# A state-space layer with a shift-mixing MLP on one core: the second mixing product from float16 halves, and a new order of the work

## The chip, the core and the metric

The kernel runs on one NeuronCore of one Trainium2 chip. The metric is device microseconds of one execution, lower is better. The kernel before takes 673.48 us (median of 3 runs, 673.35 to 673.55).

TensorE (PE) multiplies matrices, VectorE (DVE) and ScalarE (ACT) do the elementwise work, SyncE (SP) issues the transfers. Each engine works off its own instructions in order and waits on semaphores for the others.

## The reference, cut to what matters

The input is 2048 positions of 512 channels. It is normed, goes through two branches, and their product is added to it:

```
xn = layernorm(u)
# branch A: a long convolution (2048 taps for each channel)
K[d, l] = Re sum_n C[d,n] * dt[d]*B[d,n] * exp(dt[d]*A[d,n]*l)     # n = 0..127
s = irfft(rfft(pad(xn)) * rfft(pad(K))) + xn * Dskip
# branch B: shift mixing, then an MLP
h  = gelu(layernorm(xn) @ w1)          # 512 x 512
hs = concat(h quarter 0 shifted +1, 1 by -1, 2 by +2, 3 by -2) @ w2
x1 = xn + hs
h2 = gelu(layernorm(x1) @ w3) @ w4     # 512 x 1376, 1376 x 512
out = u + s * silu(x1 + h2)
```

## The kernel before

The 2048 positions stand as 16 slots of 128 in X, [128, 16, 512] float32 in SBUF.

**Branch A.** `tables(hf)` makes the powers that K is summed from. For each of 8 blocks a half (`block`, `waves`, `factors`), ACT computes exponentials (`mag`) and sines, and DVE turns them into products: `kt` and `pt` name the tables, first angles (TENSOR_SCALAR kt<-pt rounds to whole turns, pt<-kt,pt subtracts them), then sines, then sines times magnitudes. The last step are two multiplications by `mag` of each of `kt` and `pt`. Each pair of tables feeds PE: 256 small matmuls into bank pc (pc<-kt and pc<-pt, 32 weight columns, 64 wide; `sums`). What the tables of a half give is copied out (`kev`), goes through `kstage1` (k1e, to a scratch in HBM) and `products`, which reads the two spectra back (`kin`, `uin`), transforms them, multiplies them on DVE (`kh`, `pr`) and transforms back (`z1e`); the transform of u is `u_stage1` (`ue`). The last stages (`inverse`, `finish`) read a scratch as `zin`.

**Branch B.** `token_mixing` has 8 pairs of slots. `x_pair` norms and transposes two slots into xT; `h_pair` multiplies by w1 in float32 (16 matmuls of 256 columns a pair, into pb, with one gelu for each half) into hT. `hs_pair` multiplies the shifted h by w2, float32, 4 matmuls of 512 columns a slot (64 in all), into bank pa, and DVE adds that to X. The quarters of slots that wrap around are copied into `hw` by `wrapped`.

**MLP.** `mlp(g)` works on the two slots of group g, for g = 0 to 7. w3 and w4 are scaled by a power of two (found from sums of squares, `weight_squares`, `pow2_scale`) and split by `prep` into two float16 halves; the activations are split too, and each product is three float16 matmuls (high by high, and the two crossed). `mlp_input` norms two slots (x1n), transposes and splits them (x1T); then come six steps of w3 (pb<-x1T,w3h, 24 matmuls of 256 columns), gelu into g32, the split into ghl (ACT or DVE the high half, DVE the low half) and w4 (pa<-w4h,ghl, 12 matmuls of 512 columns).

**What sets the order.** No line of the program stands where it runs. All instructions are recorded into a `Plan` with what they read and write, and a due number (`due`: a stage's number, from the constants M0, H0, Q0, KA and so on, plus that stage's entry of the table SHIFT). `Plan.order` then walks a clock with modelled costs and takes for each engine, among what is ready in that model, the lowest due number. `E.affine` and `E.copy` may go to ACT or to DVE, by PREFER, AVOID and that clock. The order is fixed when the program is built; each engine's queue is what it gives, and all instructions carry the line of `issue`, L310.

**Places.** The weights' staging buffer `wst` is one buffer of 4 KB a partition: each of the 12 blocks of w3 and w4 is loaded into it once for its sum of squares and once more for `prep`. `stile` hands out the blocks that hold w1 and the eight pairs of h, `wtile` the four buffers that x2, x1n and g32 share, `vtile` two for xT and x1T.

Of the kernel before, what the change touches and what calls it, by code (L numbers as in the profile page):

```python
# [125 lines left out]
)  # L126
Q0, QC = -778.0, 0.05
SWITCH = 2279.26
PREFERP, AVOIDP = 2674.41, 272.51
PREFER, AVOID = 3332.92, 790.65  # L130
PV, T0, TC = 257.0, 396.7, 309.52
LX, LC, LP, LW, LV = -4000.0, 0.11, -3964.6, -2693.7, -3696.7
# [1117 lines left out]
```

## Time and profile before

| | before |
|---|---|
| median of 3 runs | 673.48 us |
| the profiled execution | 674.49 us |
| its span | 672.7 us |
| PE, DVE, ACT busy in it | 93%, 80%, 71% |
| granted clock of TensorE, mean | 0.97 |

The span is what the trace's instructions take from the first to the last; 1.8 us of the profiled execution lie around it, and it is 1.0 us above the median. Busy time is the share in which an engine has an instruction under way. Durations on DVE are recorded from an instruction's begin to its end, and the next one can begin before that end. A float32 matmul has two records in the trace, a float16 one or a transpose one, so the counts of records are not those of instructions.

### The profile page before, as it was taken

The page shows a single profiled execution, that of the slowest core. Times are in us where ns is not written, and L with a number is a line of the kernel's source. Part 1 is how long each engine was busy: PE and PEld are TensorE (multiplying, and loading weights), DVE is VectorE, ACT ScalarE, POOL GpSimd, SP SyncE. Part 2 cuts the span into 40 slices and gives each one's busy share as a digit, 9 for nine tenths or more (in the row PEclk, how much of TensorE's full clock was granted, in tenths as well). Part 3 has the DMA queues.
Part 4 walks back from the last instruction along what each step waited for, and adds up shares of the span by engine and source line. Part 5 has one row for each costly group of instructions (what it writes and reads, how often), then busy time and mean ns, then how long its engine had stood idle before and what let it go on. Part 6 is the DMA issues. An engine that isn't in the chain of part 4 may idle for free.

```text
span 672.7 us, 13855 instructions
## 1 busy us (share of the span) xinstructions
PE 625.8 (93%) x5526; PEld 414.4 (62%) x5526; DVE 540.7 (80%) x798; ACT 480.6 (71%) x1050; POOL 0.7 (0%) x6
## 2 busy tenths in 40 slices
PE   7489979899995999898999999999999999999984
PEld 7457858466464686665687576676675756556531
DVE  5898899999999999988999999998434154454557
ACT  3889899969938999987999999994246353223420
POOL 0000000000000000000000000000000000000000
PEclk9899999899998899998999999999999999999995
DMA  8955252422121111385343324328599568854997
GB/s 230 235 166 187 82 183 88 147 77 79 32 79 55 56 45 37 72 226 167 79 131 91 105 65 129 98 77 206 151 271 267 141 142 219 203 159 137 249 304 218
DMA packets 100751, 95.60 MB, mean 142 GB/s; under 512 B 48656, under 2 KB 81424, under 8 KB 99792
## 3 DMA queue, kind: packets, MB, share of 16 engines
q1 hardware_dynamic: 100688, 94.73, 50.3%
q8 instruction: 43, 0.70, 0.4%
q14 instruction: 20, 0.16, 0.1%
HBM read 61.16 MB, written 33.55 MB: 141 GB/s over the span
## 4 chain that ended last, share of the span: by engine, by line
PE 49%; DVE 37%; DMA 5%; ACT 4%; issue 4%; SPq 2%; DVEq 0%; ACTq 0%
PE pb L310 17%; PE pa L310 13%; DVE pt L310 11%; PE pc L310 10%; PE pd L310 9%; DVE kt L310 5%; DVE X L310 4%; DMA X<-in_A_u_dram 4%; DVE ghl L310 2%; DVE eg L310 2%; DVE pr L310 2%; DVE stats L310 2%; DVE pab L310 2%; SPq L310 2%; DVE w4h L310 1%
## 5 line engine op out<-in xcount | busy, mean ns | idle before, releaser
L310 PE MATMUL pb<-x1T,w3h 128*128 128x256 f16 (+1 forms) x1056 | 125.5, 274 | 1.2 <-DVE w3h L310 1.0
L310 PE MATMUL pa<-w4h,ghl 128*128 128x512 f16 (+1 forms) x528 | 124.5, 383 | 1.0 <-DVE w4h L310 0.8
L310 PEld LDWEIGHTS <-w3h 128*128 128x128 f16 (+1 forms) x1056 | 102.5, 101 | 30.0 <-issue 15.5
L310 ACT ACT_TABLE_LOAD x85 | 109.1, 1283 | 2.5 <-PEq L1238 0.7
L310 PEld LDWEIGHTS <-ghl 128*128 128x128 f16 (+1 forms) x528 | 49.3, 98 | 67.5 <-issue 16.5
L310 ACT ACTIVATE mag<-par 128x64 f32<-128x64 f32 x512 | 84.0, 277 | 6.5 <-DVE pt L310 6.3
L310 PE MATMUL pc<-kt 128*32 128x64 f32 x1024 | 84.1, 416 | 0.6 <-DVE kt L310 0.6
L310 PE MATMUL pc<-pt 128*32 128x64 f32 x1024 | 78.0, 388 | 0.0
L310 PE MATMUL pb<-xT,w 128*128 128x256 f32 x256 | 59.9, 390 | 2.8 <-ACT hT L310 2.8
L310 DVE SCALAR_TENSOR_TENSOR ghl<-g,wsc,ghl 128x512 f16<-128x512 f32 (+1 forms) x48 | 34.8, 733 | 31.0 <-ACT ghl L310 30.7
L310 PEld LDWEIGHTS pb<-xT,w 128*128 128x128 f32 x256 | 48.7, 194 | 15.7 <-issue 5.1
L310 PEld LDWEIGHTS pc<-pt 128*32 128x32 f32 x1024 | 56.2, 195 | 0.0
L310 PEld LDWEIGHTS pc<-kt 128*32 128x32 f32 x1024 | 48.4, 176 | 9.4 <-issue 5.9
L310 ACT ACTIVATE g<-pb,wsc 128x512 f32<-128x512 f32 (+1 forms) x48 | 32.8, 692 | 26.3 <-PE pb L310 25.9
L310 ACT ACTIVATE ghl<-g,wsc 128x512 f16<-128x512 f32 (+1 forms) x32 | 22.9, 722 | 27.1 <-PE pa L310 27.0
L310 DVE TENSOR_TENSOR kt<-mag,kt 128x1024 f32<-128x1024 f32 x32 | 40.8, 1275 | 0.0
L310 DVE SCALAR_TENSOR_TENSOR pt<-kt,pt 128x2080 f32<-128x2080 f32 x16 | 37.4, 2344 | 0.1
L310 ACT COPY z1e<-pd 128x256 f32<-128x256 f32 x36 | 12.7, 388 | 33.8 <-PE pd L310 33.8
L310 DVE TENSOR_TENSOR pr<-pc,kh 128x512 f32<-128x512 f32 x32 | 21.0, 686 | 19.4 <-PE pc L310 16.8
L310 PE MATMUL pd<-pr,cst 64*128 64x256 f32 x256 | 36.3, 402 | 0.0
L310 ACT ACTIVATE kt<-kt,halfpi 128x2080 f32<-128x2080 f32 x16 | 33.6, 2102 | 0.0
L310 DVE COPY z1e<-pd 128x256 f32<-128x256 f32 x28 | 11.6, 440 | 26.1 <-PE pd L310 26.1
(159 smaller groups left out, 981.2 us busy)
## 6 DMA issues: line engine op xcount, KB each, us to landing
wst<-in_B_w_dram SPq DMA_DIRECT2D x20, 512.0 KB, 3.8
scr_Ud<-ue SPq DMA_DIRECT2D x16, 512.0 KB, 3.3
scr_Kfa<-k1e SPq DMA_DIRECT2D x16, 256.0 KB, 3.5
uin<-scr_Ud SPq DMA_DIRECT2D x32, 128.0 KB, 3.0
cst<-c_gp SPq DMA_DIRECT2D x16, 256.0 KB, 2.6
kin<-scr_Kfa SPq DMA_DIRECT2D x32, 128.0 KB, 2.8
scr_Zda<-z1e SPq DMA_DIRECT2D x16, 256.0 KB, 2.2
xr<-in_A_u_dram SPq DMA_DIRECT2D x16, 256.0 KB, 6.4
```

The lines of the kernel that those rows point to most:

```text
L310: ins = [getattr(self.engines[op.eng], name)(*args, **kw).ins for name, args, kw in op.calls]
```

## The change

1. **The product with w2** is made of float16 halves, as the MLP's are. `h_pair` writes the gelu into g32 (a wtile), and from it the high half (ACT or DVE) and the low half (DVE, one instruction for each half pair, 16 in all) into hT. w1's sum of squares gives h's scale (`w1_scale`); w2 is loaded for its sum of squares (`w2_squares`) and again to be split (`w2_halves`). `hs_pair` has three float16 matmuls in the place of each float32 one (192 for 64), and its result is scaled as it is added to X.
2. **The sums of squares** have three staging buffers of their own (`sqt`), in the blocks that the last pairs of h are written to later, and `wst` has three buffers in the place of one. The squares are recorded after the first pair of h.
3. **The MLP** takes the groups in the order 2 to 7, 0, 1, and so do the gates, inverses and last sums; the second norm is computed in three parts.
4. **All due numbers** and the constants of the order are new.

The line of `issue` is L316 in the changed kernel.

```diff
-LAND, PAD = 2.45, 0.16
+LAND, PAD = 2.52, 0.27
+ORDER = (2, 3, 4, 5, 6, 7, 0, 1)
 SHIFT = (
-    -2357, -12777, -7728, -8471, -1890, -5820, 626, 2299, 7826, 2606, 3103, -2484, -1642, 1374, 635, 1552,
+    -41464, -36585, 6035, -36642, -5475, 685, 45975, 15018, 40059, -188, 3227, 5436, 10627, -6821, -604, 452,
...
-M0, MC, WC = 807.9, 710.86, 0.25
-H0, HC, SC = -3530.1, 638.4, 0.22
+W0 = 15894.3
+M0, MC, WC = 8607.0, 13651.7, 0.07
+H0, HC, SC = 4250.1, 0.07, 0.12
...
-    wst = Ring(early + 2 * K4, K4, 1)
+
+    sqt = Ring(sblocks + 7 * K4, K4, 3)
+    wst = Ring(early + 2 * K4, K4, 3)
     utile = Ring(early + 3 * K4, K4, 2)
...
-    hw = at(gtile.o, [P, 6, P], F32, "hw")
+    hw = at(gtile.o, [P, 6, 2, P], F16, "hw")
...
+    def w1_scale():
+        o = sblocks + K4 * 10
+        for k in range(2):
+            A.activation(
+                at(o + K4 * k, [P, 2, D], F32, "sq"), w1s[k], AF.Square, accum_out=ssq[:, 16 + k : 17 + k]
+            )
+        pow2_scale(ssq[:, 16:18], s1, i1, 2.0 ** 14)
+        V.tensor_scalar(sh, s1, 2.0 ** -10, None, op0=ALU.mult)
+        V.tensor_scalar(ih, i1, 2.0 ** 10, None, op0=ALU.mult)
+
+    def load_w2(k, ring=wst):
+        t = ring([P, 2, D], F32, "wst")
+        Q.dma_start(t, w2[2 * k * P : 2 * (k + 1) * P].rearrange("(k p) f -> p k f", p=P))
+        return t
+
+    def w2_squares():
+        for k in range(2):
+            t = load_w2(k, sqt)
+            A.activation(t, t, AF.Square, accum_out=ssq[:, 18 + k : 19 + k])
+        pow2_scale(ssq[:, 18:20], s2, i2, 2.0 ** 14)
+        V.tensor_mul(a2, ih, i2)
+
+    def w2_halves():
+        for k in range(2):
+            due(W0)
+            w = w2place([P, 2, 2, D], F16, "w2h")
+            t = load_w2(k)
+            E.affine(w[:, :, 0], t, s2)
+            V.scalar_tensor_tensor(w[:, :, 1], t, s2, w[:, :, 0], op0=ALU.mult, op1=ALU.subtract)
+            w2h.extend([w[:, 0], w[:, 1]])
...
-        t = load_w3(i) if i < 6 else load_w4(i - 6)
+        t = load_w3(i, sqt) if i < 6 else load_w4(i - 6, sqt)
...
+    HALF = ((0, 0), (0, 1), (1, 0))
+
     def h_pair(j):
-        h = stile([P, 4, 2, P], F32, "hT")
+        h = stile([P, 4, 2, 2, P], F16, "hT")
         hT.append(h)
         xT = xTs.pop(j)
         for m2 in range(2):
-            ph = mm_bank().rearrange("p (m a t) -> p m a t", m=2, a=2)
+            ph = mm_bank().rearrange("p (m t) -> p m t", m=2)
             for mi in range(2):
-                m = 2 * m2 + mi
+                m = slice((2 * m2 + mi) * P, (2 * m2 + mi + 1) * P)
                 with plan.together():
                     for k in range(4):
                         T.matmul(
-                            ph[:, mi].rearrange("p a t -> p (a t)"), w1s[k][:, m * P : (m + 1) * P],
-                            xT[:, k].rearrange("p a t -> p (a t)"), start=k == 0, stop=k == 3,
+                            ph[:, mi], w1s[k // 2][:, k % 2, m], xT[:, k].rearrange("p a t -> p (a t)"),
+                            start=k == 0, stop=k == 3,
                         )
-            A.activation(h[:, 2 * m2 : 2 * m2 + 2], ph, AF.Gelu_apprx_tanh)
+            g32 = wtile([P, 2, 2 * P], F32, "g32")
+            A.activation(g32, ph, AF.Gelu_apprx_tanh)
+            hh, hl = [h[:, 2 * m2 : 2 * m2 + 2, k].rearrange("p m a t -> p m (a t)") for k in range(2)]
+            E.affine(hh, g32, sh)
+            V.scalar_tensor_tensor(hl, g32, sh, hh, op0=ALU.mult, op1=ALU.subtract)
...
-                        w = hT[t // 2][:, m, t % 2]
+                        w = hT[t // 2][:, m, :, t % 2]
                     else:
                         w = hw[:, WRAPS.index((m, t % S))]
-                    T.matmul(acc[i], w, w2s[m], start=m == 0, stop=m == 3)
+                    for n, (lh, lw) in enumerate(HALF):
+                        T.matmul(acc[i], w[:, lh], w2h[m][:, lw], start=m + n == 0, stop=m + n == 5)
         for i in range(2):
             s = s0 + i
-            V.tensor_add(X[:, s], X[:, s], acc[i])
+            V.scalar_tensor_tensor(X[:, s], acc[i], a2, X[:, s], op0=ALU.mult, op1=ALU.add)
...
+        g = ORDER[n]
...
-            pt = t_bank() if g < 2 else mm_bank()
+            pt = t_bank() if n < 2 else mm_bank()
...
+                w1_scale()
...
                 for k in range(3, 6):
                     wrapped(k)
+                due(W0)
+                w2_squares()
+                for i in range(12):
+                    due(Q0 + QC * i)
+                    weight_squares(i)
+                weight_scales()
+            if j == 3:
+                w2_halves()
         for k in range(3):
             wrapped(k)
-        for i in range(12):
-            due(Q0 + QC * i)
-            weight_squares(i)
-        weight_scales()
         due(H0 + 8 * HC)
         prep(0)
         for k in range(8):
             due(H0 + 8 * HC + k * SC)
             hs_pair((2 * k + 2) % S, k)
+            if k == 3:
+                ln_second(slice(2, 10))
             if k in (2, 4, 6):
                 prep(len(w3t))
         while len(w3t) < 6:
             due(H0 + 8 * HC + 8 * SC + WC * len(w3t))
             prep(len(w3t))
         due(H0 + 8 * HC + 8 * SC)
-        ln_second(slice(0, S))
+        ln_second(slice(10, S))
+        ln_second(slice(0, 2))
+        due()
 
 
     due(LX)
```

The order that comes out differs on every engine. At three places, each first as it was and then as it is:

On PE, ahead of the first matmuls of the tables (kt and pt; xT is a pair's input to w1, w12 or w1 are w1's blocks, X with ks1 the transform of u), these rows before:

```order
112 L310 MATMUL pa0_93<-X_90,ks1_81 64x512
113 L310 MATMUL pa1_94<-X_90,ks1_81 64x512
114 L310 MATMUL pd0_99<-X_90,ks1_81 64x512
115 L310 MATMUL pd1_100<-X_90,ks1_81 64x512
116 L310 MATMUL pb1_96<-xT_142,w12_103 128x256 x2
117 L310 MATMUL pb1_96<-xT_142,w12_104 128x256 x2
118 L310 MATMUL pb1_96<-xT_142,w12_103 128x256 x2
119 L310 MATMUL pb1_96<-xT_142,w12_104 128x256 x2
120 L310 MATMUL pc1_98<-kt_201 32x64 x4
121 L310 MATMUL pc1_98<-pt_200 32x64 x4
```

and these in the changed kernel:

```order
50 L316 MATMUL pd0_96<-X_87,ks1_81 64x512
51 L316 MATMUL pd1_97<-X_87,ks1_81 64x512
52 L316 MATMUL pb1_93<-xT_131,w1_100 128x256 x2
53 L316 MATMUL pb1_93<-xT_131,w1_101 128x256 x2
54 L316 MATMUL pb1_93<-xT_131,w1_100 128x256 x2
55 L316 MATMUL pb1_93<-xT_131,w1_101 128x256 x2
56 L316 MATMUL pb0_92<-xT_131,w1_100 128x256 x2
57 L316 MATMUL pb0_92<-xT_131,w1_101 128x256 x2
58 L316 MATMUL pb0_92<-xT_131,w1_100 128x256 x2
59 L316 MATMUL pb0_92<-xT_131,w1_101 128x256 x2
60 L316 MATMUL pc1_95<-kt_220 32x64 x4
61 L316 MATMUL pc1_95<-pt_219 32x64 x4
```

The first matmul of the tables is row 120 of PE before, behind six and a half pairs of h (104 matmuls with w1), and row 60 now, behind three pairs (48).

On DVE, the first rounding of angles and what stands around it (hT is h, g32 the gelu's result, wsc the scales) in the changed kernel:

```order
117 L316 TENSOR_TENSOR pt_224<-par_89,ev_84 128x1056
118 L316 TENSOR_TENSOR pt_219<-pab_217 128x1024
119 L316 TENSOR_SCALAR hT_134<-g32_135,wsc_79 128x2x256
120 L316 TENSOR_SCALAR kt_220<-pt_219 128x2080
121 L316 SCALAR_TENSOR_TENSOR hT_134<-g32_135,wsc_79,hT_134 128x2x256
122 L316 COPY wsc_79<-pd1_97 128x1
123 L316 SCALAR_TENSOR_TENSOR pt_219<-kt_220,pt_219 128x2080
124 L316 TENSOR_SCALAR wsc_79<-wsc_79 128x1
125 L316 COPY wsc_79<-pd0_96 128x1
126 L316 SCALAR_TENSOR_TENSOR hT_134<-g32_136,wsc_79,hT_134 128x2x256
```

and the same place before:

```order
122 L310 TENSOR_TENSOR pt_205<-par_92,ev_84 128x1056
123 L310 TENSOR_SCALAR x2_149<-X_90,rs_74 128x512
124 L310 COPY par_92<-pc0_97 128x256
125 L310 TENSOR_TENSOR pab_198<-pab_198,par_92 128x256
126 L310 TENSOR_TENSOR EB_196<-EB_196,par_92 128x256
127 L310 TENSOR_TENSOR pt_200<-pab_198 128x1024
128 L310 TENSOR_TENSOR eg_202<-EB_196 128x1024
129 L310 TENSOR_TENSOR pt_205<-pab_198 128x1024
130 L310 TENSOR_TENSOR pab_212<-par_92,ev_84 128x768
131 L310 SCALAR_TENSOR_TENSOR pt_200<-kt_201,pt_200 128x2080
```

The halves of h and the arithmetic on the scales stand between the tables' steps on DVE, and the rounding (row 120) is on DVE where it was on ACT before.

On SP's queue, after the last of the small parameters (ld), before:

```order
9 L310 DMA ld_85<-in_A_log_dt_dram 128x4x1
10 L310 DMA w12_103<-in_B_w1_dram 128x2x512
11 L310 DMA w12_104<-in_B_w1_dram 128x2x512
12 L310 DMA ks1_81<-c_ks1 128x64
13 L310 DMA X_90<-in_A_u_dram 32x2048 x4
```

and in the changed kernel:

```order
9 L316 DMA ld_85<-in_A_log_dt_dram 128x4x1
10 L316 DMA wst_119<-in_B_w3_dram 128x4x256
11 L316 DMA X_87<-in_A_u_dram 32x1024 x4
12 L316 DMA X_87<-in_A_u_dram 32x2048 x8
13 L316 DMA w1_100<-in_B_w1_dram 128x2x512
14 L316 DMA w1_101<-in_B_w1_dram 128x2x512
```

The two loads of w1 stand behind a block of w3 and ten slots of X now.

## Rows read from the trace of the kernel before

**Rows 1.** The page's first two parts: busy us; 40 slices of the span.
```profile
PE 625.8 (93%) x5526; PEld 414.4 (62%) x5526; DVE 540.7 (80%) x798; ACT 480.6 (71%) x1050; POOL 0.7 (0%) x6
...
DVE  5898899999999999988999999998434154454557
...
GB/s 230 235 166 187 82 183 88 147 77 79 32 79 55 56 45 37 72 226 167 79 131 91 105 65 129 98 77 206 151 271 267 141 142 219 203 159 137 249 304 218
```

**Rows 2.** Windows: stretch, length, busy PE, PEld, DVE, ACT, POOL (count), clock, DMA, GB/s.
```profile
0.00:162.10 162.10, 140.65 (x1111) 105.58 (x1111) 144.89 (x262) 137.12 (x344) 0.70 (x6) 0.97 0.50 149
162.10:460.00 297.90, 284.57 (x2735) 192.33 (x2735) 291.94 (x345) 269.33 (x589) 0.00 (x0) 0.98 0.33 93
460.00:652.40 192.40, 191.83 (x1572) 114.12 (x1569) 88.86 (x169) 73.09 (x118) 0.00 (x0) 1.00 0.76 205
652.40:672.70 20.30, 8.78 (x113) 2.42 (x112) 14.96 (x25) 1.06 (x1) 0.00 (x0) 0.60 0.75 210
```

**Rows 3.** Timeline of DVE: start, us, engine, line, operation, out<-in, shape.
```profile
91.56 1.22 DVE L310 TENSOR_TENSOR kt<-mag,kt 128x1024 f32<-128x1024 f32 x1
92.70 1.22 DVE L310 SCALAR_TENSOR_TENSOR pt<-mag,pt 128x1024 f32<-128x1024 f32 x1
...
458.67 1.23 DVE L310 SCALAR_TENSOR_TENSOR pt<-mag,pt 128x1024 f32<-128x1024 f32 x1
```

**Rows 4.** Timeline of PE; in brackets the wait ahead and who ended it.
```profile
16.21 7.22 PE L310 MATMUL pb<-xT,w 128*128 128x256 f32 x32
...
73.71 10.53 PE L310 MATMUL pb<-xT,w 128*128 128x256 f32 x48
...
161.49 0.61 PE L310 MATMUL pc<-pt 128*32 128x64 f32 x8
162.03 14.00 PE L310 MATMUL pa<-w,hT 128*128 128x512 f32 x32
...
216.40 1.97 PE L310 MATMUL pd<-ident,x1n 128*128 128x128 f32 x8 [6.79 <-ACT x1n L310]
...
219.76 1.11 PE L310 MATMUL pd<-ident,x1n 128*128 128x128 f32 x4 [1.39 <-ACT x1n L310]
...
231.24 5.34 PE L310 MATMUL pa<-w4h,ghl 128*128 128x512 f16 x24
...
460.60 0.67 PE L310 MATMUL pc<-kt 128*32 128x64 f32 x8
```

**Rows 5.** Groups of DVE by shape: xcount | busy us, mean ns | idle before, releaser.
```profile
L310 DVE SCALAR_TENSOR_TENSOR ghl<-g,wsc,ghl 128x512 f16<-128x512 f32 x40 | 31.1, 785 | 27.7 <-ACT ghl L310 27.4
...
L310 DVE SCALAR_TENSOR_TENSOR X<-pa,wsc,X 128x512 f32<-128x512 f32 x16 | 12.0, 787 | 0.0
...
L310 DVE TENSOR_SCALAR kt<-pt 128x2080 f32<-128x2080 f32 x8 | 10.5, 1311 | 0.1
...
L310 DVE TENSOR_TENSOR X<-X,pb 128x512 f32<-128x512 f32 x8 | 7.0, 894 | 0.4 <-PE pb L310 0.4
L310 DVE TENSOR_SCALAR ghl<-g,wsc 128x512 f16<-128x512 f32 x13 | 6.8, 525 | 2.4 <-PE pa L310 1.9 <-ACT g L310 0.5
L310 DVE SCALAR_TENSOR_TENSOR w3h<-wst,wsc,w3h 128x1024 f16<-128x1024 f32 x5 | 6.4, 1281 | 0.0
...
L310 DVE TENSOR_TENSOR X<-X,pa 128x512 f32<-128x512 f32 x8 | 5.9, 752 | 0.0
...
L310 DVE COPY ue<-pd 128x512 f32<-128x512 f32 x8 | 5.5, 715 | 0.0
...
L310 DVE COPY kev<-pc 128x256 f32<-128x256 f32 x9 | 4.3, 474 | 0.0
...
L310 DVE TENSOR_SCALAR w3h<-wst,wsc 128x1024 f16<-128x1024 f32 x2 | 1.5, 732 | 0.0
```

**Rows 6.** Groups of PE by shape, in the same columns.
```profile
L310 PE MATMUL pb<-x1T,w3h 128*128 128x256 f16 x960 | 114.0, 275 | 0.2
...
L310 PE MATMUL pc<-kin,cst 128*64 128x256 f32 x128 | 17.2, 390 | 0.0
```

More of the change, by code (lines that the diff above doesn't have):

```diff
@@ L102 @@
 WARM = 40
+ORDER = (2, 3, 4, 5, 6, 7, 0, 1)
 SHIFT = (
[21 rows of a table removed]
[L126 to L137 removed]
[24 rows of a table added]
+)
+W0 = 15894.3
+Q0, QC = -9250.6, 0.12
+SWITCH = 30545.2
+PREFERP, AVOIDP = 12844.2, 10831.3
+PREFER, AVOID = 27556.6, 25513.7
+PV, T0, TC = 13567.5, 13842.2, 2940.7
+LX, LC, LP, LW, LV = -4000.0, 0.06, 1841.0, 8563.3, -8160.3
+M0, MC, WC = 8607.0, 13651.7, 0.07
+H0, HC, SC = 4250.1, 0.07, 0.12
+KA, PA, PAC, FA = -22322.5, -14370.0, 0.13, 32880.5
+KB, PB, PBC, FB = 2597.0, 23920.3, 0.24, 2934.7
+FC = 0.51
 def mlp_due(g, jp):
@@ L481 @@
     warm = keep([P, 1], "warm")
[L482 to L483 removed]
+    wsc = keep([P, 24], "wsc")
+    ssq = keep([P, 24], "ssq")
     ks1 = keep([P, 2 * NG], "ks1")
@@ L488 @@
     ld = keep([P, 4], "ld")
-    mxs = [keep([P, 1], "mx") for _ in range(2)]
-    m1s = [keep([1, 1], "m") for _ in range(2)]
+    mx8 = keep([P, 8], "mx")
+    mxs, m1s = [mx8[:, k : k + 1] for k in range(4)], [mx8[0:1, k : k + 1] for k in range(4, 8)]
     assert place[0] <= FINE
@@ L598, in loads @@
         due(LW)
-        load_w(w1, w1s, stile)
+        for k in (0, 2):
+            w = stile([P, 2, D], F32, "w1")
+            Q.dma_start(w, w1[k * P : (k + 2) * P].rearrange("(k p) f -> p k f", p=P))
+            w1s.append(w)
         Q.dma_start(ks1, c_ks1)
@@ L886, in products, with gate, inverse @@
             )
-    def gate(g):
-        due(FA + FC * g)
+    def gate(pos):
+        due(FA + FC * pos)
+        g = ORDER[pos]
         X2 = X[:, 2 * g : 2 * g + 2]
         A.activation(X2, X2, AF.Silu)
-    def inverse(hf, g):
-        due((FA, FB)[hf] + FC * g)
+    def inverse(hf, pos):
+        due((FA, FB)[hf] + FC * pos)
+        g = ORDER[pos]
         ch = slice(hf * DH, hf * DH + DH)
@@ L909, with finish @@
     xr = []
-    def finish(g):
-        due(FB + FC * g)
-        if g % 2 == 0:
+    def finish(pos):
+        due(FB + FC * pos)
+        g = ORDER[pos]
+        if pos % 2 == 0:
             xr.append(at(xrs.pop(), [P, 4, D], F32, "xr"))
@@ L936, in pow2_scale, with load_w3, load_w4 @@
         V.tensor_scalar(dst_inv, dst_inv, 1.0 / float(target), None, op0=ALU.mult)
-    s3, i3, s4, i4, sg, ig, a3, a4 = [wsc[:, k : k + 1] for k in range(8)]
+    s3, i3, s4, i4, sg, ig, a3, a4, s1, i1, s2, i2, sh, ih, a2 = [wsc[:, k : k + 1] for k in range(15)]
     w3t, w4t = [], []
-    def load_w3(jp):
+    def w1_scale():
[25 more added lines that the diff above has]
+            w2h.extend([w[:, 0], w[:, 1]])
+    def load_w3(jp, ring=wst):
         n = min(2 * P, F - jp * 2 * P)
-        t = wst([P, 4, 2 * P], F32, "wst")
+        t = ring([P, 4, 2 * P], F32, "wst")
         Q.dma_start(t[:, :, :n], w3[:, jp * 2 * P : jp * 2 * P + n].rearrange("(k p) f -> p k f", p=P))
         return t[:, :, :n]
-    def load_w4(jp):
-        t = wst([P, 2, D], F32, "wst")
+    def load_w4(jp, ring=wst):
+        t = ring([P, 2, D], F32, "wst")
         if jp < 5:
@@ L1105, in mlp_input, with mlp @@
             V.tensor_sub(x1T[:, 1, :, i * P : (i + 1) * P], pv, x1T[:, 0, :, i * P : (i + 1) * P])
-        x1Ts[g] = x1T
-    def mlp(g):
-        x1T = x1Ts.pop(g)
+        x1Ts[n] = x1T
+    def mlp(pos):
+        g = ORDER[pos]
+        x1T = x1Ts.pop(pos)
         accs = bank[0]
         for jp in range(6):
-            due(mlp_due(g, jp))
+            due(mlp_due(pos, jp))
             if jp == 3:
-                mlp_input(g + 1)
+                mlp_input(pos + 1)
             js = [j for j in (2 * jp, 2 * jp + 1) if j < len(FT)]
@@ L1188, in token_mixing @@
         due(H0 + 8 * HC + 8 * SC)
-        ln_second(slice(0, S))
+        ln_second(slice(10, S))
+        ln_second(slice(0, 2))
+        due()
     due(LX)
```

31 lines of the change are left out of this document (10 added, 21 removed), and 43 rows, old and new, of the table SHIFT.

## The prediction

> **What bounds the kernel now.** I read the page's busy shares first, then the slices, then windows cut where the trace changes its character, and last the timelines of the two engines at the cuts. The page alone says TensorE: 93% busy [rows 1]. The slices say that VectorE stands at 9 or at 8 until about slice 27 and falls to 5 and below then. The windows [rows 2] say the same in numbers. From 162.1 to 460.0 us VectorE is busy 291.94 of 297.90, so it has 6.0 us to spare, and TensorE has 13.3. From 460.0 to 652.4 TensorE has 0.6 us to spare, and VectorE more than half of the time. What ends at 460 is the tables: the last multiplication by mag begins at 458.67 and takes 1.23, so it ends at 459.9 [rows 3], and the first matmul on it starts at 460.60 [rows 4]. So the kernel has two limits, one behind the other. VectorE sets when the tables are done; what TensorE then has left sets the rest. TensorE's high share before 460 is other work that was put into its waits.
>
> The time of before, worked out this way: 459.9 + 0.7 + 212.1 (from 460.60 to the span's end) = 672.7. The profiled execution took 674.49, 1.8 more than its span, and the median is 1.0 below that one; so measured = span + 0.8.
>
> **Prices.** VectorE's recorded durations are a little longer than the stride: two table steps begin 1.14 apart where 1.22 is recorded [rows 3], so I take 0.08 off each mean. A float32 matmul of 512 columns counts twice in the records: 14.00 for 32 records is 0.875 an instruction [rows 4], I take 0.86; a float16 one of that shape takes 5.34 / 24 = 0.2225. A matmul of h: 10.53 for 24 instructions, 0.439.
>
> **The product with w2 on TensorE.** It removes 64 × 0.86 = 55.0 and adds 192 × 0.2225 = 42.7: 12.3 less. The price of the new ones is that of w4's matmuls, the same shape and type with weights that change as often. If each new weight load showed as well, by 114.12 / 1569 = 0.073 [rows 2], three would take 0.886 and the change would lose 1.7 here instead. I take 12.3, since w4's rows are back to back.
>
> **What VectorE does up to the last table step.** I compared its order up to that multiplication with the order before, and priced what is new there and what is gone by [rows 5]. New:
> - 16 low halves of h, as the MLP's at 785 ns: 16 × 0.705 = 11.3.
> - 5 of the 16 high halves (the others go to ACT), as ghl's at 525: 5 × 0.445 = 2.2.
> - w2's halves: 2 × 1.2 (as w3's at 1281) and one high half, half as long: 3.0.
> - Roundings kt<-pt: 21 on VectorE where there were 14: 7 × 1.23 = 8.6.
> - Additions to X: 24 with a scale (787) for 16 without (894 and 752) and 6 with: 17.0 for 15.8, 1.2.
> - Copies kev, 16 for 8: 8 × 0.39 = 3.1. Copies kh and xT, 5 more, taken as ue's (715): 5 × 0.635 = 3.2.
> - MLP and product steps that now stand ahead: two low halves 1.4, three x1n (as the 525 row) 1.3, two groups of spectrum products, an estimate of 2.1 (three full passes' worth).
> - Scales of w1, w2 and h, maxima, and the second norm in three parts: some 20 small instructions, an estimate of 3.
>
> That is 40.4. Gone from there: 10 ue and 2 k1e at 0.635, 7.6; 4 norms x and 3 high halves ghl at 0.445, 3.1; four high halves of w3 and w4 (732) at about 0.65, 2.6; smaller copies, 1.6. That is 14.9. The balance is **25.5 us more** on VectorE ahead of the table's end, where 23.2 us in all were free: 17.2 up to 162.1 and 6.0 after [rows 2].
>
> **Sum A, from the tables' end.** With the idle time of before, the last step ends at 459.9 + 25.5 = 485.4. TensorE then has less left, since more is done ahead of it: 36 of w4's matmuls × 0.2225 = 8.0; 12 of w3's × 0.119 (114.0 / 960 [rows 6]) = 1.4; 8 of kin's and uin's × 0.27 (17.2 us for 64 instructions [rows 6]) = 2.2; 4 of pr's, taken as these, 1.1; 8 transposes of x1n, 1.2. Sum 13.9. The tail of 20.3 us after the last MLP matmul [rows 2] has five groups to read and add back where it had seven: I take 2 off, between 0 and 20.3 × 2 / 7 = 5.8. The span is 485.4 + 0.7 + 212.1 − 13.9 − 2 = **682.3**.
>
> **Sum B, from the fourth pair of tables.** An early check with other rows. Before, TensorE ends the fourth pair at 162.1, with 140.65 us of work done [rows 2], all of h and 24 matmuls of the first product among them, and hs goes on at once [rows 4]. Now w1 comes after 3.0 MB more of w3 and X; at 230 GB/s [rows 1] that is 13 us, and the first h matmul goes from 16.21 to about 30. VectorE has 5.3 us more ahead of the fourth pair's end, so TensorE is there at 167.4, and it has more left than it had: 24 h matmuls × 0.439 = 10.5, and all of hs, 42.7, where 40 × 0.86 = 34.4 were left: 8.3. The other way go the waits for x1n at the second norm, 6.79 and 1.39 [rows 4], since that norm is computed in parts while hs runs: 8.2, and the 2 of the tail. 167.4 + 510.6 + 10.5 + 8.3 − 8.2 − 2 = **686.6**.
>
> The two sums are 4 apart; I take a span of 685, which is **685.8** measured.
>
> **Bounds.** The term that decides is idle time on VectorE up to the end of the tables. By sum A, idle of 0 instead of 23.2 would be a span of 659; half of it filled, 670.7; twelve more than before (the 13 us by which h is late, if nothing else is ready then) 694. I take it as before, since VectorE waits in the first stage for loads and the parameters, which remain. The new wst and sqt rings let loads start early; they hide behind tables at a DMA share of 0.33 [rows 2], so I cost them at nothing, and the second load of w2 likewise; without that cover its 1 MB would be 4.5 us at 230 GB/s. The new group order by itself changes no count of matmuls: nothing. New due times on ACT, which is busy 269.33 of 297.90 there, can give back at most the 28.6 us that it is idle, and cost as much where VectorE waits for it.
>
> **Rivals.**
> - *TensorE is the limit (faster).* TensorE has the highest busy share [rows 1]; then the 12.3 us saved come off the time: 661.2. For it to hold, the tables must end by 460.4 + 0.6 or so, with 25.5 us more on VectorE: all of its idle time would have to go. For any gain over 0.2%, idle must fall below about 11 of the 23. Against it stand the 6.0 in 297.9. For it: the roundings are moved to VectorE off ACT, so a later wait for ACT may be gone. Chance 0.14.
> - *The two cancel (no change).* Twelve of VectorE's free microseconds are filled by the finer mix of halves and tables, and the time is 673 to 674. Chance 0.08.
> - *TensorE waits more (slower still).* After the tables x1T's halves, ghl's and zin's adds share VectorE with the last w3 and w4 halves; if the waits for x1n stay at 8.2, sum B gives 694.8, 695.6 measured. It decides where the second norm's last two parts come after the last hs. Chance 0.15.
> - *The halves don't save.* Weight loads show, 14.0 more on TensorE; since it is not the limit before the tables' end, half of that would come through: 692. Chance 0.02.
>
> The Trainium skill, "Perfetto Trace Analysis", section "Identifying the Most-Contended Engine", says that the engine with the highest occupancy is the most contended and is to be optimized first, and that for TensorE matmul busy time is no good measure of the room left. By its first half the change aims at the right engine, and the time would be the first rival's 661.2; by its second half the 93% says little, and the window of 291.94 busy in 297.90 on VectorE decides. The trace of before bears out the second.
>
> **How the numbers follow.** Likeliest, the tables end 20 to 30 us later and the time is 677 to 693, point 685.8: 0.61. The range of 8 in 10 leaves out some 0.1 at each end: below 668 lies most of the first rival, above 697 half of the third. What a measurement can tell from no change is about 0.2%, 1.35 us: faster than 672.1 has 0.14, within has 0.08, slower has 0.61 + 0.15 + 0.02 = 0.78.
>
> **What would show it.** Right: the last multiplication by mag ends near 485 and VectorE is busy over 97% between the fourth pair and it; the fourth pair's matmuls end near 167; hs takes about 43 us of TensorE; the stretch from the tables' end to the span's end is near 197. Wrong: tables that end before 472, with VectorE idle under 11 us up to there; table steps that take less time each than the 1.22 of before; or a stretch after the tables over 205, which would make the end a matter of TensorE's waits.

## The result, and the profile after

The changed kernel takes 677.93 us (median of 5 runs, 676.89 to 679.01) against 673.54 for the kernel before: **0.5% slower**, ratio 1.0049 with a 95% interval of 1.003 to 1.0068. The forecast was slower by 12 us; it is slower by 3.3 (by the ratio) to 4.4 (by the medians). That lies just inside the stated 677 to 693, at about a third of the forecast change.

The page's first two parts of the changed kernel, which answer to [rows 1]:

```profile
PE 611.7 (90%) x5596; PEld 410.7 (61%) x5596; DVE 559.4 (83%) x839; ACT 492.0 (73%) x1080; POOL 0.7 (0%) x6
...
PE   7364399899899899999999999999999999999993
...
DVE  5899999999999999999999999989545335555456
```

and TensorE's slices before:

```profile
PE   7489979899995999898999999999999999999984
```

TensorE has 14 us less to do and VectorE 19 more. TensorE's new waits are in slices two to five, some 17 to 85 us: 3, 6, 4, 3 where it had 4, 8, 9, 9. VectorE has no slice below 9 from the third to the twenty-sixth.

Windows of the changed kernel, cut where TensorE fills up, where the tables end, and at the last matmul with w4, in the columns of [rows 2] (stretch, length, busy us and count of PE, PEld, DVE, ACT and POOL, TensorE's granted clock, DMA share, GB/s):

```profile
0.00:166.60 166.60, 119.35 (x1036) 95.68 (x1036) 155.23 (x272) 150.42 (x381) 0.70 (x6) 0.85 0.46 139
166.60:479.66 313.06, 305.95 (x2962) 205.02 (x2954) 306.85 (x389) 272.35 (x586) 0.00 (x0) 0.99 0.36 101
479.66:659.90 180.24, 180.06 (x1538) 108.29 (x1540) 86.10 (x162) 68.17 (x114) 0.00 (x0) 1.00 0.79 215
659.90:676.90 17.00, 6.34 (x81) 1.72 (x80) 11.19 (x19) 1.06 (x1) 0.00 (x0) 0.59 0.67 186
```

The tables end at 479.66, where they ended at 459.9; these are the last multiplications by mag on VectorE's timeline, for [rows 3]:

```profile
477.30 1.22 DVE L316 SCALAR_TENSOR_TENSOR pt<-mag,pt 128x1024 f32<-128x1024 f32 x1
478.44 1.22 DVE L316 TENSOR_TENSOR kt<-mag,kt 128x1024 f32<-128x1024 f32 x1
```

And TensorE's timeline where [rows 4] were read: the first h matmuls, the first matmuls of the tables, a piece of the product with w2, and the first matmul on the last tables.

```profile
28.01 8.86 PE L316 MATMUL pb<-xT,w 128*128 128x256 f32 x32 [12.45 <-DMA w<-in_B_w_dram]
...
92.40 0.71 PE L316 MATMUL pc<-kt 128*32 128x64 f32 x8
...
179.21 5.34 PE L316 MATMUL pa<-w2h,hT 128*128 128x512 f16 x24 [0.74 <-ACT ue L316]
...
481.24 0.66 PE L316 MATMUL pc<-kt 128*32 128x64 f32 x8
```

The waits for x1n of [rows 4] are gone. 24 float16 matmuls of the product take 5.34 us, as those with w4 do.

Every window up to the tables' end gives VectorE's busy time and, by subtraction, its idle time; the rest of the span lies behind. All times are of one profiled execution each. The runs of one kernel spread over 1 to 6 us (the kernel before, beside the experiments, took 672.2 to 678.5), so that a microsecond between two rows says little:

| kernel | VectorE busy | idle | tables end | from there | span |
|---|---|---|---|---|---|
| before | 436.7 | 23.2 | 459.9 | 212.8 | 672.7 |
| forecast (first sum) | 462.2 | 23.2 | 485.4 | 196.9 | 682.3 |
| changed | 462.1 | 17.6 | 479.7 | 197.2 | 676.9 |

Two of the three terms came out within 0.3 us. Idle time did not, by 5.6.

### The profile page after: what moved, and what is told of

Read it like the earlier page. It is cut to its first block, busy times and chain, and to the rows that moved or that the text cites. A ratio compares the mean times of both kernels' runs of the same rounds, so it can differ in the third digit from the quotient of the medians.

```text
span 676.9 us, 14055 instructions
## 1 busy us (share of the span) xinstructions
PE 611.7 (90%) x5596; PEld 410.7 (61%) x5596; DVE 559.4 (83%) x839; ACT 492.0 (73%) x1080; POOL 0.7 (0%) x6
## 4 chain that ended last, share of the span: by engine, by line
PE 53%; DVE 23%; ACT 10%; DMA 7%; issue 4%; SPq 3%; DVEq 0%; ACTq 0%
PE pb L316 17%; PE pa L316 13%; PE pc L316 12%; PE pd L316 10%; DVE pt L316 7%; DMA X<-in_A_u_dram 3%; DVE kt L316 3%; DVE X L316 3%; SPq L316 3%; ACT mag L316 2%; ACT L316 2%; DVE stats L316 1%; DMA zin<-scr_Zdb 1%; DMA is<-c_is 1%; ACT EB L316 1%
## 5 line engine op out<-in xcount | busy, mean ns | idle before, releaser
L316 PE MATMUL pb<-x1T,w3h 128*128 128x256 f16 (+1 forms) x1056 | 123.5, 273 | 0.6 <-DVE x1T L316 0.4
L316 PE MATMUL pa<-w4h,ghl 128*128 128x512 f16 (+1 forms) x528 | 121.6, 380 | 0.0
L316 PEld LDWEIGHTS <-w3h 128*128 128x128 f16 (+1 forms) x1056 | 101.9, 100 | 26.4 <-issue 14.7
L316 PEld LDWEIGHTS <-ghl 128*128 128x128 f16 (+1 forms) x528 | 49.5, 98 | 62.9 <-issue 10.8
L316 ACT ACTIVATE mag<-par 128x64 f32<-128x64 f32 x512 | 82.3, 260 | 6.6 <-DVE kt L316 4.1
L316 PE MATMUL pc<-kt 128*32 128x64 f32 x1024 | 83.6, 417 | 1.8 <-ACT kev L316 1.8
L316 PE MATMUL pc<-pt 128*32 128x64 f32 x1024 | 77.5, 389 | 0.4 <-DVE pt L316 0.4
L316 PE MATMUL pb<-xT,w 128*128 128x256 f32 x256 | 62.1, 400 | 15.8 <-DMA w<-in_B_w_dram 12.5
L316 PEld LDWEIGHTS pb<-xT,w 128*128 128x128 f32 x256 | 50.4, 201 | 28.2 <-issue 15.7
L316 ACT ACTIVATE g<-pb,wsc 128x512 f32<-128x512 f32 (+1 forms) x48 | 33.0, 696 | 33.6 <-PE pb L316 32.8
L316 PEld LDWEIGHTS pc<-pt 128*32 128x32 f32 x1024 | 55.6, 196 | 0.8 <-DVE pt L316 0.7
L316 PEld LDWEIGHTS pc<-kt 128*32 128x32 f32 x1024 | 47.9, 177 | 13.0 <-issue 9.2
L316 DVE SCALAR_TENSOR_TENSOR ghl<-g,wsc,ghl 128x512 f16<-128x512 f32 (+1 forms) x48 | 35.2, 741 | 20.7 <-ACT ghl L316 20.3
L316 DVE SCALAR_TENSOR_TENSOR pt<-kt,pt 128x2080 f32<-128x2080 f32 x16 | 41.1, 2567 | 0.2
L316 DVE TENSOR_TENSOR kt<-mag,kt 128x1024 f32<-128x1024 f32 x32 | 40.7, 1271 | 0.0
L316 ACT ACTIVATE ghl<-g,wsc 128x512 f16<-128x512 f32 (+1 forms) x36 | 25.2, 700 | 18.9 <-PE pa L316 18.4
L316 ACT COPY z1e<-pd 128x256 f32<-128x256 f32 x39 | 13.6, 384 | 33.9 <-PE pd L316 32.8
L316 PE MATMUL pd<-pr,cst 64*128 64x256 f32 x256 | 36.3, 402 | 0.1
L316 DVE TENSOR_TENSOR pr<-pc,kh 128x512 f32<-128x512 f32 x32 | 20.7, 686 | 17.6 <-PE pc L316 14.4
L316 ACT ACTIVATE kt<-kt,halfpi 128x2080 f32<-128x2080 f32 x16 | 32.5, 2029 | 0.0
L316 ACT ACTIVATE pt<-pt 128x2080 f32<-128x2080 f32 x16 | 32.1, 2008 | 0.2
```

The source lines that it names most:

```text
L316: ins = [getattr(self.engines[op.eng], name)(*args, **kw).ins for name, args, kw in op.calls]
```

## The experiments

Each was run beside the kernel before on the same chip; ratios are to that kernel, with 95% intervals, so the changed kernel stands at 1.0049, and microseconds between two changed kernels are differences of ratios times 674.5. The diffs are shortened to what they do. Where the text says that the order is held, every engine has the changed kernel's instructions (or those of before) in the same order, apart from the edit.

**1. Less on VectorE, on TensorE, on both.** The low halves of h cut to 16 columns (first diff), the 64 crossed matmuls that read them taken out (second), and both. Where the low halves are cut or unused, the kernel's product leaves that term out.

```diff
+ if op.idx in low_halves:            # at issue
+     out, g32, hh = out[:, :, :8], g32[:, :, :8], hh[:, :, :8]
```
```diff
- HALF = ((0, 0), (0, 1), (1, 0))     # what is issued, the plan unchanged
+ HALF = ((0, 0), (0, 1))
```

> The changed kernel in its own order on every engine, with the 16 low halves of h cut to 16 columns each and the crossed matmuls that read them given the high half instead (so the product lacks that term). VectorE has 16 x 0.6 = 9.6 us less, TensorE and ScalarE the same. Theory A (the prediction's: VectorE's work up to the tables' end sets the time, one for one): the tables end at 469 instead of 478.5 and the time falls by 8 to 10 us, to 668 to 670. Theory B (what the two traces say together: the loss lies in the opening, where TensorE waits 47.3 us up to 166.6 for VectorE's first tables with too few h pairs ahead of them, and behind it TensorE has only 7.1 us of waits left, so both engines are full): the opening is shorter by the 9 or 10 low halves that stand ahead of the fourth pair of tables, some 5 us, and TensorE gives no more than 2 of its waits behind it: 671 to 673.

> The changed kernel in its own order, without the 64 crossed matmuls that read h's low halves, which are still made (the product lacks that term). TensorE has 64 x 0.22 = 14.2 us less, VectorE the same. If TensorE alone is the limit behind the opening: 664 to 667. Theory A: VectorE still ends the tables at 478.5, and the time falls only by what TensorE was late then, 2.8 us, and by nothing after it: 675. Theory B says the same of this one, since both engines are full: 674 to 676.

> Both edits together: VectorE has 9.6 us less and TensorE 14.2 (h's low halves are neither made nor used). Theory A: 668 to 670, as without the low halves. Theory B, both engines full behind 166.6: the opening gives 5, and behind it the smaller of what the two have less, some 4 to 5: 667 to 669, which is more than the sum of the two single edits' gains only if one hid the other.

Measured: 0.9997 (0.9976 to 1.0018) without the low halves, 1.0047 (1.0026 to 1.0069) without the 64 matmuls, 0.9986 (0.997 to 1.0001) without both. All three times lie above what any theory had expected. So some 8 us off VectorE gave 3.5, and 64 matmuls off TensorE gave nothing. TensorE's waits between 166 and 480 us with the matmuls taken out (engine, line, waited for: us in total, times, longest):

```profile
PE pb L316 <- DVE X L316: 8.4, 4, 4.0
PE pa L316 <- DVE X L316: 6.1, 6, 3.1
```

TensorE's busy time from 166.6 to 260 fell by 11.3 (88.81 to 77.47), and these waits for VectorE's additions to X, which free the two banks, rose from 3.9 to 14.5: what was saved was waited out. "TensorE alone is the limit" is refuted. The single-engine view of VectorE, one for one, is refuted too: without the low halves VectorE's busy time up to the tables' end fell by 8.0, but its idle time rose by 4.8, and they end only 3.2 earlier (476.4).

**2. The scale chains, and ScalarE's squares.** Scales as constants; then the squares cut to 16 or 32 columns as well; then the low halves cut too.

```diff
- pow2_scale(ssq[:, 16:18], s1, i1, 2.0 ** 14)     # and the other three
+ V.memset(s1, 2.0 ** 15); V.memset(i1, 2.0 ** -15)
```

> The changed kernel in its own order with the four power-of-two scales written as constants in place of the chains that find them (squares on ScalarE and their loads stay; the maxima, transposes, square roots and copies go). In the changed kernel's opening TensorE waits 12.4 us for ScalarE's square roots and 5.1 for VectorE's copies of the scales. Rival S (these waits in TensorE's queue are what the change lost): 664 to 668. Theory B: the first tables come when VectorE has them, and only the chains' small instructions on VectorE, some 3 us, and the switches of ScalarE's tables come off: 673 to 676. Theory A: 3 us off too, 674 to 676.

> The kernel with constant scales, same order, and its 16 sums of squares on ScalarE cut to a few columns each (their loads stay): ScalarE has some 13 us less, nearly all of it before 100 us. Against the kernel with constant scales alone (2 to 3 us under the changed kernel): theory C, both engines full in the opening, so that one alone gives little: 2 to 4 us more, 671 to 674. If ScalarE alone sets the opening: 8 or more, 664 to 668. Theory A: nothing more, 675.

> The same, and the 16 low halves of h cut to 16 columns as well (the crossed matmuls take the high half instead, so the product lacks that term): ScalarE has 13 us less and VectorE 9.6 + 3. Theory C: both of the opening's full engines have less, so more than the sum of the single edits' gains: 664 to 668. Theory A: VectorE's alone, as the two single edits on it, 671. If TensorE, full behind 166.6, sets the time: only what the opening gives, some 8, 668 to 670.

Measured: 1.0014 (0.9997 to 1.003), 1.003 (1.0015 to 1.0045), 0.9951 (0.9936 to 0.9967). The 17.5 us of TensorE's waits in these chains were worth what their small steps on VectorE are, 2.4 us. Taking 10.2 us off ScalarE on top (406.5 us busy up to the tables' end for 416.7) gave nothing. So the theory that two engines were full and shared the limit is refuted as well: ScalarE was busy, but the work taken off it was not waited for. With VectorE relieved of both, the tables end at 471.9, and the time is the 671 expected of VectorE's share alone.

**3. w1 earlier.** The two loads put back to their old place in the queue, the order held otherwise.

```diff
+ first = the two loads of w1
+ for op in rest[:at] + first + rest[at:]:     # at: the first load of w3
```

> The changed kernel in its own order, with the two loads of w1 put back to where they stood before on the queue of transfers: ahead of the block of w3 and the ten slots of X. In the changed kernel TensorE waits 12.5 us for w1, and its first h matmul starts at 28.0. Rival L (the late w1 costs, the step of the prediction's second sum): h starts at 16 to 19 and the time falls by 8 or more, to 667 to 670. Theory C (from 50 to 166 us VectorE and ScalarE are both full, 116.4 and 113.1 of 116.6, and what TensorE does early only waits for the first tables): within 2 us of the changed kernel, 676 to 680, the first matmul of the tables still at 92 or a little later, since X comes 4 to 5 us later.

Measured: 1.0097 (1.0059 to 1.0136), some 3 us slower than the changed kernel, though the two intervals overlap a little; neither expectation had that. The first h matmul starts at 16.4 instead of 28.0, and TensorE then waits 20.8 us for VectorE's x of the next pair. VectorE's waits for X grow from 6.9 to 8.8 us, and it idles 21.5 us instead of 17.6. So the late w1 cost nothing; the bound of 694 had priced it at 12 us.

**4. VectorE loaded in the kernel before.** Sixteen instructions like the low halves, the order held.

```diff
+ vector.scalar_tensor_tensor(junk, h, 2.0, h, op0=ALU.mult, op1=ALU.subtract)   # six VectorE instructions behind each gelu
```

> The kernel before in its own order, with 16 instructions put in on VectorE, one behind each half pair's gelu, that do what the low halves do (512 columns of h in, 512 of float16 out, to a place that nothing reads). 16 x 0.62 to 0.70 us is 10 to 11 us more on VectorE; no other engine has anything new. Theory A (VectorE's work up to the tables' end counts one for one, its idle time stays): 683 to 685. Theory C (VectorE's waits for TensorE in the opening, 5.7 us between 50 and 100 and around it, take some of it up): 678 to 681.

Measured: 1.0078 (1.0059 to 1.0098), 5 us. The tables end 4.5 us later for some 9 us of work (16 recorded at 682 ns): VectorE's idle time fell from 23.2 to 19.0. Half of added work was free here, as part of it was in the change.

**5. TensorE relieved in the kernel before.** Three of four matmuls of the product taken out, the order held.

```diff
- T.matmul(acc[i], w, w2s[m], start=m == 0, stop=m == 3)   # m = 0..3
+ T.matmul(acc[i], w, w2s[0], start=True, stop=True)
```

> The kernel before in its own order, with one of the four float32 matmuls of each group of the product with w2 (the other three quarters of its sum are left out): TensorE has 48 x 0.86 = 41 us less, no other engine anything less. If what the product takes on TensorE is on the path (the whole point of float16 halves): 12 us or more faster, under 661. If VectorE, which waits for nothing in that stretch before (97.83 busy of 97.90), sets the tables' end: the tables end at 459 to 460 as before, TensorE waits the 41 us out, and the time is 671 to 674.

Measured: 1.0013 (0.9995 to 1.0031). 48 matmuls off an engine that is 93% busy changed nothing. The window up to the tables' end of this kernel:

```profile
0.00:460.95 460.95, 395.60 (x3747) 283.65 (x3748) 436.82 (x606) 405.62 (x931) 0.70 (x6) 0.92 0.39 112
```

VectorE's 436.82 and the idle 24.1 are those of before within 1 us; TensorE's busy time fell by 30 up to there and its waits rose by as much (not by the 41 forecast: from 162 to 260 us, where it waits more, its granted clock fell from 0.95 to 0.83, and the product's matmuls that are left have 0.69 to 0.88 us a record for 0.59). What the product cost on TensorE was not on the path, so making it cheaper could not pay.

**6. The product alone, the order alone.** Three tries: the changed kernel's order held with the float32 product; the float32 product planned under the new due numbers; the halves planned under the old ones.

```diff
- A.activation(g32, ph, AF.Gelu_apprx_tanh)      # and the halves of h and w2, and their scales
+ A.activation(h32, ph, AF.Gelu_apprx_tanh)
- 12 float16 matmuls of a group
+ 4 float32 matmuls
```

> The changed kernel's own order held on every engine, but the product with w2 in float32 again: gelu writes h in float32, the low and high halves of h and w2 and the scales of w1 and w2 with their squares and loads are taken out where they stood, and each group of 12 float16 matmuls is 4 float32 ones. VectorE has some 16 us less, ScalarE 14, TensorE 12.3 more. What remains of the change is its order of the work, its staging and its groups. Theory A (VectorE's work one for one): 660 to 664. Theory C (VectorE and ScalarE both full in the opening, VectorE's additions pacing the product): the opening gives 6 to 9, and 12.3 more on TensorE behind it is felt only in part, since the product's stretch waits for VectorE's additions anyway: 673 to 680. Under 672 would say that the order gains by itself and the product from halves costs more than the whole change lost.

> The changed kernel, planned with its own due numbers and constants, with the product with w2 as it was: float32, no halves of h and w2, no scales of w1 and w2 (the order of the groups, the staging and the due numbers are the changed kernel's, and the planner fits them to fewer instructions). VectorE has 17 to 19 us less, ScalarE about 14, TensorE 12.3 more. Theory A: 659 to 664. Theory C: the opening gives some 8 to 10 us, since both of its full engines have less, and TensorE, full behind it, gives most of that back: 674 to 681. If the product alone is the change's loss and the order neither gains nor loses: 673.

> The kernel before, planned with its own due numbers and constants, with the product with w2 from float16 halves (w1's and w2's scales and halves and three matmuls for one; no other part of the change). VectorE has 17 to 19 us more, ScalarE 14, TensorE 12.3 less. TensorE as the limit: 661. Theory A: 688 to 691. Theory C: what TensorE saves is worth nothing, since its product waits for VectorE's additions to X, and both full engines of the opening have more: 683 to 690. Below 680 would say that the new due numbers and staging lose time and the product does not.

Measured: 1.0104 (1.0076 to 1.0132), 1.0426 (1.0385 to 1.0467), 1.0995 (1.0944 to 1.1045). All three expectations missed, the first by 1.6 us. The last two say how narrowly due numbers fit one set of instructions: with another set, planned anew, the same numbers lose 29 and 67 us, so they price neither part. The first is readable. VectorE has 16 us less up to the tables' end (446.0), and they end 2.9 us later, because its idle time is 36.6. Its waits between 166 and 260 us:

```profile
DVE X L327 <- PE pa L327: 6.4, 8, 1.0
DVE X L327 <- PE pb L327: 4.8, 3, 2.0
DVE w4h L327 <- ACT w4h L327: 1.5, 2, 1.1
DVE w3h L327 <- PE pb L327: 0.4, 1, 0.4
```

In the changed kernel the same stretch has 0.4 us of waits in all, 0.2 of them for X. In this order, then, the float16 product gains 3.7 us: it takes 11 us of waiting for the product out of VectorE, and gives it its halves to do instead.

**7. Low halves on GpSimd.** The order held, two steps in the place of one.

```diff
- vector.scalar_tensor_tensor(hl, g32, sh, hh, op0=ALU.mult, op1=ALU.subtract)
+ gpsimd.tensor_scalar(g32, g32, sh, None, op0=ALU.mult)
+ gpsimd.tensor_tensor(hl, g32, hh, op=ALU.subtract)
```

> The changed kernel in its own order, with the 16 low halves of h made on GpSimd, which does nothing else there, in two steps each (scale, subtract). VectorE has 16 x 0.6 to 0.7 us less. If GpSimd takes nothing from VectorE: as without the low halves, 3 to 4 us less than the changed kernel, 674 to 675. If its steps slow VectorE's own instructions while they run, part or all of that is lost: 676 to 682.

Measured: 1.0216 (1.0188 to 1.0244), 11 us slower than the changed kernel and above the 676 to 682 expected. VectorE has 16 instructions less and is busy 462.7 us up to the tables' end, no less than with them, and waits 10.1 us for GpSimd's halves. The rows are under the last heading.

**8. Roundings on ScalarE.** Nine of the eleven float32 ones that the planner gave to VectorE (the expectation says eight; the trace has two left), the order held.

```diff
- vector.tensor_scalar(kt, pt, MAGIC, None, op0=ALU.add)
+ scalar.activation(kt, pt, AF.Identity, bias=magic, scale=1.0)
```

> The changed kernel in its own order, with 8 of the 9 or so roundings of angles that the planner gave to VectorE done on ScalarE at the same places of the order: VectorE has 8 x 1.23 = 9.8 us less, ScalarE 8 x 1.95 = 15.6 more, TensorE the same. At the rate the runs so far show (0.3 to 0.55 us at the tables' end for one of VectorE's): 673 to 675. If the balance between the two engines is what the new order lost, with ScalarE idle for 40 us behind 166.6: 668 to 671. If ScalarE's queue holds the tables up instead: 678 or more.

Measured: 1.0229 (1.0201 to 1.0258), 12 us slower. VectorE's busy time fell by 12.6, its idle time rose by 21.7 to 39.3, and the first of these waits up to the tables' end is most of it (the second is 2.9 in the changed kernel):

```profile
DVE pt L320 <- ACT kt L320: 19.8, 7, 4.5
DVE pt L320 <- ACT pt L320: 4.0, 4, 1.3
```

A rounding is recorded with 1.33 us on VectorE in the changed kernel and with 2.11 on ScalarE here. VectorE waits up to 4.5 for one, so part of that wait is for what stands ahead of it in ScalarE's order. The Trainium skill, "Perfetto Trace Analysis", section "Optimizing Scalar/DVE Operations", says that when VectorE is saturated, moving some work to ScalarE may make sense. Here ScalarE had 40 us free behind 166.6, and the move lost 12.

**9. A version.** h kept as one float16 value, so that the low halves, the split and w1's scale fall away; w2 keeps both halves. The product is rounded once more than in the changed kernel. With the roundings on ScalarE in a second kernel.

```diff
- A.activation(g32, ph, AF.Gelu_apprx_tanh)     # and E.affine(hh, ...), V.scalar_tensor_tensor(hl, ...)
+ A.activation(hh, ph, AF.Gelu_apprx_tanh)
- for lh, lw in ((0, 0), (0, 1), (1, 0)):
+ for lw in (0, 1):
```

> A version: the changed kernel in its own order, with h kept as one float16 value (gelu writes it so, with no scale) and w2 in halves: no low halves of h, no split, no scale of w1, two matmuls in the place of three. VectorE has 14 us less, ScalarE 11, TensorE 14.2. Idle time of VectorE taken as constant: 664. At the rates so far: the tables end at 470 to 473 and the time is 669 to 672, faster than both kernels.

> That version with the 8 roundings on ScalarE as well: VectorE has 24 us less than in the changed kernel up to the tables' end, ScalarE about 5 more, TensorE 14.2 less. If the edits add up at the rates so far: 664 to 669.

Measured: 669.93 us, 0.9934 (0.991 to 0.9958), faster than both kernels; and 1.0179 (1.0153 to 1.0204) with the roundings moved, 16.5 us slower than the version, where the same move had cost 12 and 664 to 669 us were expected (22.0 us of waits for ScalarE's kt). The version's window up to its tables' end:

```profile
0.00:470.58 470.58, 412.41 (x3923) 295.91 (x3923) 449.95 (x629) 413.29 (x950) 0.70 (x6) 0.94 0.40 116
```

VectorE's busy time is 12.1 under the changed kernel's, its idle time 3.1 over it, and the tables end 9.1 earlier.

**All whose order was held, by the three terms**, up to the tables' end and behind it:

| kernel | VectorE busy | idle | tables end | from there | span |
|---|---|---|---|---|---|
| before | 436.7 | 23.2 | 459.9 | 212.8 | 672.7 |
| before, 16 more on VectorE | 445.4 | 19.0 | 464.4 | 212.7 | 677.1 |
| before, a quarter of the product | 436.8 | 24.1 | 460.9 | 213.1 | 674.0 |
| changed | 462.1 | 17.6 | 479.7 | 197.2 | 676.9 |
| no low halves | 454.1 | 22.3 | 476.4 | 196.8 | 673.2 |
| 64 matmuls less | 461.8 | 17.3 | 479.1 | 197.2 | 676.3 |
| both | 453.5 | 22.3 | 475.8 | 196.9 | 672.7 |
| constant scales | 459.6 | 17.4 | 477.0 | 197.5 | 674.5 |
| constant scales, short squares | 459.5 | 17.8 | 477.3 | 198.0 | 675.3 |
| those and no low halves | 451.2 | 20.8 | 471.9 | 197.1 | 669.0 |
| w1 first | 461.9 | 21.5 | 483.4 | 196.8 | 680.2 |
| float32 product, order held | 446.0 | 36.6 | 482.6 | 197.4 | 680.0 |
| halves on GpSimd | 462.7 | 27.8 | 490.6 | 197.3 | 687.9 |
| roundings on ScalarE | 449.5 | 39.3 | 488.8 | 197.2 | 686.0 |
| h in one float16 | 450.0 | 20.6 | 470.6 | 196.8 | 667.4 |
| the same, roundings on ScalarE | 436.4 | 52.1 | 488.4 | 196.8 | 685.2 |

The last but one column stays within 1.2 us in an order, 212.7 to 213.1 and 196.8 to 198.0. The differences within an order are VectorE's busy and idle time.

## Why the prediction was right, and where it was wrong

**Right: where the limit is.** "VectorE sets when the tables are done; what TensorE then has left sets the rest." Taking 48 matmuls from TensorE ahead of the tables' end (experiment 5) and 64 of the shorter ones (experiment 1) changed nothing, and the stretch behind it did not move in any kernel of one order.

**Right: the two counted terms.** VectorE's extra work, 25.5 forecast, is 25.4 (462.08 less 436.73). Some of its parts, by shape up to the tables' end in the changed kernel:

```profile
L316 DVE SCALAR_TENSOR_TENSOR pt<-kt,pt 128x2080 f32<-128x2080 f32 x16 | 41.1, 2567 | 0.2
L316 DVE TENSOR_SCALAR kt<-pt 128x2080 f32<-128x2080 f32 x11 | 14.7, 1332 | 0.0
L316 DVE TENSOR_SCALAR kt<-pt 128x2080 int32<-128x2080 int32 x10 | 13.0, 1304 | 0.0
L316 DVE SCALAR_TENSOR_TENSOR hT<-g,wsc,hT 128x512 f16<-128x512 f32 x16 | 11.7, 754 | 0.0
L316 DVE COPY kev<-pc 128x256 f32<-128x256 f32 x16 | 6.7, 418 | 0.0
```

The low halves came to 16 × (0.754 − 0.08) = 10.8, for 11.3. That the whole comes as near as 0.1 us is in part luck: the 16 subtractions pt<-kt,pt, which the list of the forecast does not have, take 3.7 us more than in the kernel before,

```profile
L310 DVE SCALAR_TENSOR_TENSOR pt<-kt,pt 128x2080 f32<-128x2080 f32 x16 | 37.4, 2344 | 0.1
```

and other steps take less time each. What TensorE has left behind the tables is 15.6 less, for 15.9 forecast. The product itself came out as priced: its records add up to 46.1 us where they were 58.7, 12.6 less for 12.3.

**Wrong: the idle time.** The step was: "The term that decides is idle time on VectorE up to the end of the tables... I take it as before, since VectorE waits in the first stage for loads and the parameters, which remain." Part of those waits were not for loads. VectorE's waits up to 162.1 us, before:

```profile
DVE stats L310 <- DMA X<-in_A_u_dram: 8.4, 4, 3.6
DVE ue L310 <- PE pd L310: 2.4, 2, 2.1
DVE x L310 <- PE pd L310: 1.8, 1, 1.8
DVE xT L310 <- PE pd L310: 1.6, 1, 1.6
...
```

and in the changed kernel:

```profile
DVE stats L316 <- DMA X<-in_A_u_dram: 6.9, 4, 3.7
DVE rawA L316 <- ACT mag L316: 1.4, 1, 1.4
...
DVE par L316 <- PE pc L316: 0.6, 1, 0.6
DVE xT L316 <- PE pd L316: 0.3, 1, 0.3
```

Before, 6.8 us of the opening's idle time were waits for TensorE (5.8 in ue, x and xT, the rest in two shorter ones) and 9.0 for loads. In the changed kernel 0.9 and 7.8 are left, and 1.4 for ScalarE is new. At 56 to 70 us, where VectorE had waited 4.2 us for ue and x, its order now has halves of h, scales and roundings. The 1.6 us for xT lay at 11 to 13 us, ahead of any half of h, so that the new order, not the added work, brought them to 0.3. That added work fills idle time, and that work taken away leaves it, is shown by the experiments: of 8.7 us more in the kernel before, 4.2 came out of idle time (4), and of 8.0 less in the changed one, 4.8 went back into it (1).

The prediction read the sum of the idle time and not its waits. With the 5.8 us taken as filled, the first sum would have been 676.5 for 676.9 measured; that it comes so near is in part luck, since the shorter waits for loads and the new one for ScalarE set each other off.

**Wrong: the second sum,** and with it the choice of 685 over 682.3. It put TensorE's end of the fourth pair at 167.4: 162.1 and VectorE's 5.3 us more. TensorE ended that pair at 158.5. The windows up to the pair's last multiplication by mag, before and in the changed kernel:

```profile
0.00:153.22 153.22, 131.77 (x977) 98.63 (x978) 136.01 (x244) 128.57 (x304) 0.70 (x6) 0.97 0.52 155
```
```profile
0.00:152.40 152.40, 105.20 (x868) 83.74 (x868) 141.06 (x259) 136.31 (x326) 0.70 (x6) 0.83 0.49 149
```

and TensorE's first matmuls on that pair before, then its wait for the pair and its last matmuls in the changed kernel:

```profile
155.61 0.67 PE L310 MATMUL pc<-kt 128*32 128x64 f32 x8
```
```profile
152.45 0.62 PE L316 MATMUL pc<-pt 128*32 128x64 f32 x8 [0.45 <-DVE pt L316]
...
157.94 0.60 PE L316 MATMUL pc<-pt 128*32 128x64 f32 x8
```

VectorE's extra work is 5.05 there, as counted, but its idle time is 11.3 for 17.2, the same step as above; and TensorE, which before came to the pair 2.4 us after its tables were done, now waited for them. Behind the fourth pair the sum held: 518.4 us for 519.2.

**The rivals.** "TensorE is the limit" fell with experiment 5. "The two cancel" named the right mechanism (VectorE's free time filled by the mix of halves and tables) with too much of it, 12 us where it was 5.6. "TensorE waits more" did not come: from 166.6 to the tables' end TensorE has 7.1 us of waits in 313.06, none of them for x1n, and from the tables' end to the span's end it is 197.2 us. "The halves don't save" is refuted by the 5.34 us for 24.

**What stays open.** The change's parts are not priced apart. In the new order the halves gain 3.7 us over float32; what the new order and staging would cost under a float32 product with due numbers fitted to it was not tried. Why a given order leaves VectorE 17 or 23 us idle is shown wait by wait for the opening only.

## What to carry to other kernels

Split the time at the point where the limiting engine changes, into its busy time, its idle time, and what the other engine has left; busy time can be counted from the order. Idle time is no constant: look at each of its waits. Those for other engines gave most of the room for added work here (6.8 us before, 0.9 for TensorE in the changed kernel, 4.5 in experiment 4); those for loads gave less (9.0, 7.8 and 7.5). Before work is taken off an engine, look whether anything waits for it in the stretch where that work stands: the busiest engine of the page may be filling in.
